# Attention of one query over a long cache: keys loaded and scored one pair ahead of the values

## The chip, the core and the metric

The kernel runs on one core of one Trainium2 chip. The metric is the time of the kernel on the device in microseconds (us), as the median of several runs. A profile is one further execution that was recorded; its span, from the first to the last instruction, is a little shorter than the time of a run.

The engines have short names in what follows: PE multiplies matrices and transposes them, DVE, ACT and POOL work elementwise (ACT also computes the exponentials, POOL the reductions over partitions), and SP issues the loads. SP's loads form one queue, which 16 DMA engines serve in order.

## What is computed

There are 32 query heads of one position each, and 8 heads of keys and values with 65536 positions of 128 numbers; four query heads share one head of keys and values. In bf16, keys and values are 134 MB each.

```python
B, Hq, Hkv, Sq, Sk, D = 1, 32, 8, 1, 65536, 128
k = jnp.repeat(k, rep, axis=1)
v = jnp.repeat(v, rep, axis=1)
scores = jnp.einsum("bhqd,bhkd->bhqk", q, k) * D ** -0.5
p = jax.nn.softmax(scores, axis=-1)
return jnp.einsum("bhqk,bhkd->bhqd", p, v)
```

## The kernel before

**Tiling.** A head's 65536 positions are cut into four units of 128 tiles; a tile is 128 positions by 128 numbers. Two units make a *pair*, so there are 16 pairs, two to a head, numbered p = 0 to 15 (`NP`). The keys of a pair, K(p), are 8 MB, and so are its values, V(p). A unit within a pair is called n = 0 or 1.

**Buffers.** `kbuf` holds the keys of a whole pair (64 KB on each partition), `bbuf` those of one unit. `vbuf` holds the values of one pair; there is one such buffer. `pts` holds the exponentials of a unit (one buffer for each n), `qkb` in PSUM the scores of a unit, `pvb` the sums of values.

**What happens to a pair.** For each of 16 groups of 8 tiles PE transposes the keys (L135), DVE or ACT copies the transposes from PSUM to `ktb` (L207, L205), and PE multiplies them with the four queries (L144), three groups behind the transposes. Unit 1 is read from `bbuf`: while PE works on unit 0, POOL copies six and ACT two sixteenths-of-a-pair from the second half of `kbuf` to `bbuf` (`copy_unit`, L213), so that `kbuf` comes free early. When a unit's scores are complete, DVE takes the maximum over its positions (L225), POOL takes it over the partitions (L393), DVE forms the new running maximum (L235, L236, L243), and ACT the exponentials with their sums (L347) and the factor alpha by which what was summed so far has to shrink (L351). Then PE multiplies the exponentials with the values (`pe_values`, L162): 128 matmuls for each unit, one group of accumulation in PSUM for each, in `pvb[0]` and `pvb[1]`. DVE adds each group to `acc` (L257, L259). At the end of a head the sum of the exponentials is reduced on POOL (L395), and the quotient is written (L309; L305 in the last head).

**The order of the work** is written out by hand, engine by engine, with semaphores. On PE a lap of the loop is the transposes and scores of both units, and then the values of both units of the same pair (`pe_pair`). On SP the order is K0, V0, K1, V1, ..., K15, V15. Three semaphores hold loads back:

- `kfree` (L411, L418, L428, L407): K(p) waits until unit 0 of pair p-1 is transposed and unit 1 copied to `bbuf`: three counts a pair.
- `bfree`: keys that are loaded straight into `bbuf` (pairs 0, 14 and 15, which are loaded by units; the others, `WHOLE`, are loaded as a whole) wait until unit 1 of the pair before is transposed.
- `vfree` (L437, or L407 for the last pair's pieces): V(p) waits until PE is done with the values of pair p-1. DVE counts it up when the last group of values is complete (`pvd`).

K0 is loaded in four pieces and V15 in five (128, 73, 38, 13 and 4 tiles), each with a semaphore of its own; all other values have one semaphore for the whole load. In the last lap of PE, L155 adds `acc` to the last group by a matmul with the identity, so that only the quotient is left after it.

Of the kernel before, what the change touches and what calls it, by code (L numbers as in the profile page):

```python
# [5 lines left out]
DT = mybir.dt  # L6
# [24 lines left out]
WHOLE = (1, 14)  # L31
# [20 lines left out]
def bass_standalone__gqa_softmax__decode_kernel(nc, q, k, v, out):  # L52
# [32 lines left out]
    cmax = sb("cmax", [P, R], DT.float32)  # L85
# [5 lines left out]
    rsum = sb("rsum", [P, R], DT.float32)  # L91
# [25 lines left out]
    acr, l_sem, lws = sem("acr"), sem("l_sem"), sem("lws")  # L117
    xd, xa, xg = sem("xd"), sem("xa"), sem("xg")
# [19 lines left out]
    def pe_scores(pe, n, j):  # L138
        take(pe, eva if on_act(j) else evd)
        if n == 0 and j == 0:  # L140
            take(pe, qrdy)
        for i in range(TB):
            t, off = j * TB + i, (j % NKG * TB + i) * P
            ins = pe.matmul(qkb[n][:, t * R:(t + 1) * R], lhsT=ktb[:, off:off + P],  # L144
                            rhs=qcur[:, :], start=True, stop=True)
        if j == G - 1:
            ins.then_inc(qkd, 1)

    def pe_values(pe, n, lap):
        vv = vbuf[:, n * T * D:(n + 1) * T * D].rearrange("p (t d) -> p t d", d=D)  # L150
        for t in range(T):
            if n and t == V_PIECES[1][0]:
                with pe.If(lap == NP - 1):
                    pe.wait_ge(acr, H)
                    pe.matmul(pvb[n][:, 0:R], lhsT=identf[:, :], rhs=acc[:, :], start=False, stop=False)  # L155
            if t == 0:
                take(pe, vp[n][0], 16)
                take(pe, exd)
# [3 lines left out]
            ins = pe.matmul(pvb[n][:, 0:R], lhsT=vv[:, t, :], rhs=pts[n][:, t * R:(t + 1) * R],  # L162
                            start=t == 0, stop=t == T - 1)
            if piece:
                pe.sem_inc(piece, -16)
        ins.then_inc(pvd, 1)

    def pe_pair(pe, lap):
# [9 lines left out]
        for n in range(2):  # L178
            pe_values(pe, n, lap)
# [44 lines left out]
    def chunk_max(e, n):  # L224
        e.tensor_reduce(cmax[:, :], qkb[n][:, :].rearrange("p (t g) -> p g t", g=R),  # L225
                        AX.X, ALU.max).then_inc(cm, 1)

    def new_max(e, n, fresh):
        take(e, cma)

        mn, mo = m[n], m[1 - n]

        def newer(to):
            if fresh:
# [4 lines left out]
        if fresh:  # L239
            newer(mn).then_inc(dmr, 1)  # L240
        else:
            own(e, newer(mn), xd)
            e.tensor_tensor(dm[:, :], mn[:, :], mo[:, :], ALU.subtract).then_inc(dmr, 1)  # L243

    def rescale(e, n, fresh):
        take(e, sx)
        if fresh:
            own(e, e.tensor_copy(lp[:, :], rsum[:, :]), xd)
        else:
            own(e, e.tensor_tensor(acc[:, :], acc[:, :], alpha[:, :], ALU.mult), xd)  # L250
            own(e, e.tensor_tensor(lp[:, :], lp[:, :], alpha[:, :], ALU.mult), xd)
            own(e, e.tensor_tensor(lp[:, :], lp[:, :], rsum[:, :], ALU.add), xd)

    def values_done(e, n, fresh):
        e.wait_ge(pvd, 1)
        if fresh:
            own(e, e.tensor_copy(acc[:, :], pvb[n][:, 0:R]), xd)  # L257
        else:
            own(e, e.tensor_tensor(acc[:, :], acc[:, :], pvb[n][:, 0:R], ALU.add), xd)  # L259
        e.sem_inc(pvd, -1)  # L260

    def dve_pair(e, second, lap):

        fresh, last = not second, second
        for j in range(G):
            if not on_act(j):
                evict(e, 0, j)
            if j == 0:
                e.sem_inc(pgo, 1)
        for j in (0, 1, 2):  # L270
            evict(e, 1, j)
        take(e, qkd)
        chunk_max(e, 0)
        evict(e, 1, 4)
        new_max(e, 0, fresh)
        for j in (5, 6, 8, 9, 10):
            evict(e, 1, j)
        rescale(e, 0, fresh)
        if fresh:
            own(e, e.tensor_copy(otmp[:, 0:HR - R], oT[:, R:HR]), xd)  # L280
            own(e, e.tensor_copy(oT[:, 0:HR - R], otmp[:, 0:HR - R]), xd)
            e.transpose(orow[:, :], oT[:, :]).then_inc(t_o, 1)
        for j in (12, 13, 14):
            evict(e, 1, j)
        take(e, qkd)
        chunk_max(e, 1)
        new_max(e, 1, False)
        if last:
# [3 lines left out]
        values_done(e, 0, fresh)  # L292
        rescale(e, 1, False)
        if not last:
            e.wait_ge(pvd, 1)
            e.sem_inc(vfree, 1)
            values_done(e, 1, False)
            return
        e.sem_inc(acr, 1)
# [3 lines left out]
        with e.If(lap == H - 1):  # L303
            e.wait_ge(pvd, 1)
            e.tensor_tensor(oT[:, HR - R:HR], pvb[1][:, 0:R], recip[:, :], ALU.mult).then_inc(t_f, 1)  # L305
        with e.Else():
            e.wait_ge(pvd, 1)
            e.sem_inc(vfree, 1)
            own(e, e.tensor_tensor(acc[:, :], acc[:, :], pvb[1][:, 0:R], ALU.add), xd)  # L309
            e.tensor_tensor(oT[:, HR - R:HR], acc[:, :], recip[:, :], ALU.mult).then_inc(t_f, 1)  # L310
        e.sem_inc(pvd, -1)
# [16 lines left out]
    def vector_engine(e):  # L328
# [6 lines left out]
        with e.Fori(0, H) as lap:  # L335
            dve_pair(e, False, lap)
            dve_pair(e, True, lap)
        e.wait_ge(s_x, 2)
# [3 lines left out]
    def exps(e, n):  # L342
        take(e, ng)
        sv = qkb[n][:, :].rearrange("p (t g) -> p g t", g=R)
        pv = pts[n][:, :].rearrange("p (t g) -> p g t", g=R)
        for g in range(R):
            ins = e.activation(pv[:, g, :], sv[:, g, :], AF.Exp, bias=negm[:, g:g + 1],  # L347
                               scale=scale, accum_out=rsum[:, g:g + 1])
        ins.then_inc(exd, 1)
        take(e, dmr)  # L350
        e.activation(alpha[:, :], dm[:, :], AF.Exp, scale=1.0).then_inc(sx, 1)  # L351

    def act_pair(e, lap):
# [10 lines left out]
        for j in (3, 7):  # L364
            evict(e, 1, j)
        exps(e, 0)
        for j in (11, 15):
            evict(e, 1, j)
        exps(e, 1)

    def scalar_engine(e):
# [3 lines left out]
        e.activation(identf[:, :], ident[:, :], AF.Copy).then_inc(t_if, 1)  # L375
        with e.Fori(0, NP) as lap:
# [3 lines left out]
    def gpsimd_engine(e):  # L380
# [3 lines left out]
        with e.Fori(0, H) as lap:  # L384
            for u in range(HU):
                if u % 2 == 0:
                    take(e, pgo)
                    lo, hi = ((w - u // 2 + 1) // 2 for w in WHOLE)
                    cond = (lap - (lo - 1)) * (hi - lap) > 0 if lo else lap < hi
                    copy_unit(e, cond, POOL_COPIES, e.tensor_copy, cpg, xg)  # L390
                    e.sem_inc(kfree, 1)
                take(e, cm)
                e.partition_all_reduce(cmaxa[:, :], cmax[:, :], P, bass.bass_isa.ReduceOp.max).then_inc(cma, 1)  # L393
# [4 lines left out]
    def sync_engine(e):  # L398
# [14 lines left out]
        for p in range(NP):  # L413
            ks, vs = src(kf, p), src(vf, p)
# [5 lines left out]
            else:  # L420
                for n in range(2):
                    if n and p:
                        e.wait_ge(bfree, p)
                    to, s = bbuf if n else kbuf, ks[:, n * W:(n + 1) * W]
                    if p == 0 or (p == NP - 1 and n == 0):
                        pieces(to, s, K_PIECES[n], kp[n])
                    else:
                        e.dma_start(to[:, 0:W], s).then_inc(kp[n][0], 16)  # L428
                        tokens(kp[n][1:])
                e.sem_inc(cpg, len(POOL_COPIES))  # L430
                e.sem_inc(cpa, len(sum(ACT_COPIES.values(), ())))
            if p:
                e.wait_ge(vfree, p)
            if WHOLE[0] <= p < WHOLE[1]:
                tokens(kp[1])
# [6 lines left out]
        e.wait_ge(t_o, H)  # L442
# [43 lines left out]
```

## Time and profile before

| | |
|---|---|
| median of 3 runs | 628.17 us (628.1 to 628.23) |
| span of the profiled execution | 626.9 us |
| PE busy | 484.6 us, 77% |
| DVE busy | 315.1 us, 50% |
| ACT busy | 228.9 us, 37% |
| POOL busy | 159.9 us, 26% |
| queue of loads, share of the 16 DMA engines' time | 99.2% |
| read from memory | 268.44 MB, 428 GB/s over the span |

A row of the timeline or of a group names the line (L162 is line 162 of the kernel before), the engine, the operation, the tile written and the tiles read, and how many. The idle time before a row stands in brackets, with what ended it; "PEq" or "DVEq" there is the engine's own sequencer, which is also where a wait for a DMA can show. An issue of a load has as its time to landing the time until the last of its 16 parts is in. Busy time of PE says how long matmuls were under way and not that PE was at its peak.

### The profile page before, as it was taken

How to read it: one execution, taken by the hardware profiler on the slowest of the kernel's cores; microseconds unless marked ns; L12 is line 12 of the kernel's file. 1: busy time of each engine (PE TensorE's matmuls, PEld its weight loads, DVE VectorE, ACT ScalarE, POOL GpSimd, SP SyncE). 2: the span in 40 equal slices, each digit the busy share in tenths (PEclk: the TensorE clock that was granted, in tenths of full speed). 3: DMA queues.
4: the chain of work that ended last, by engine and by line, in shares of the span. 5: the costliest groups of instructions: out<-in, count | busy, mean ns of one | idle time of the engine just before them, and what ended most of it. 6: DMA issues, size and time to landing. Idle time of an engine off the chain costs nothing. (4 is left out here: it accounts for less than half of the span.)

```text
span 626.9 us, 27931 instructions
## 1 busy us (share of the span) xinstructions
PE 484.6 (77%) x12340; PEld 478.9 (76%) x12340; DVE 315.1 (50%) x699; ACT 228.9 (37%) x445; POOL 159.9 (26%) x124
## 2 busy tenths in 40 slices
PE   5752995959859498694976959679496894999698
PEld 5752995949859498694976959679496894999698
DVE  4620752817537174371734717356183562848274
ACT  2320532615335153341634407245062441624133
POOL 0000704307042070520605115060150702400000
PEclk9965875958769587695966959678596785969597
DMA  8999999999999999999999999999999999999997
GB/s 366 440 449 424 439 431 439 431 439 426 443 422 447 410 460 410 460 406 460 410 439 431 426 443 426 443 426 439 431 439 431 439 431 435 416 447 424 420 433 302
DMA packets 6280, 268.57 MB, mean 428 GB/s; under 512 B 896, under 2 KB 1024, under 8 KB 1152
## 3 DMA queue, kind: packets, MB, share of 16 engines
q1 hardware_dynamic: 6224, 268.45, 99.2%
q8 instruction: 6, 0.10, 0.1%
q10 hardware_dynamic: 48, 0.01, 0.0%
q14 instruction: 2, 0.02, 0.0%
HBM read 268.44 MB, written 0.01 MB: 428 GB/s over the span
## 5 line engine op out<-in xcount | busy, mean ns | idle before, releaser
L207 DVE COPY ktb<-trb 128x1024 bf16<-128x1024 bf16 x384 | 254.6, 689 | 177.5 <-PE trb L135 173.7
L205 ACT ACTIVATE ktb<-trb 128x1024 bf16<-128x1024 bf16 x128 | 131.0, 1023 | 352.7 <-PE trb L135 297.9
L135 PE MATMUL trb<-ident,kbuf 128*128 128x128 bf16 x2048 | 177.1, 245 | 104.7 <-PEq L49 104.6
L135 PEld LDWEIGHTS trb<-ident,kbuf 128*128 128x128 bf16 x2048 | 143.9, 111 | 105.6 <-issue 105.5
L213 POOL COPY bbuf<-kbuf 128x2048 bf16<-128x2048 bf16 x78 | 143.9, 1893 | 177.6 <-POOLq L49 177.6
L144 PE MATMUL qkb<-qcur,ktb 128*128 128x4 bf16 x4096 | 174.3, 165 | 11.8 <-PEq L49 10.3
L144 PEld LDWEIGHTS qkb<-qcur,ktb 128*128 128x128 bf16 x4096 | 155.2, 97 | 14.6 <-issue 14.6
L135 PE MATMUL trb<-ident,bbuf 128*128 128x128 bf16 x2048 | 157.0, 220 | 5.2 <-issue 3.9
L162 PE MATMUL pvb<-pts,vbuf 128*128 128x4 bf16 x4096 | 113.0, 166 | 15.2 <-PEq L49 11.0
L162 PEld LDWEIGHTS pvb<-pts,vbuf 128*128 128x128 bf16 x4096 | 111.1, 103 | 16.6 <-issue 15.6
L135 PEld LDWEIGHTS trb<-ident,bbuf 128*128 128x128 bf16 x2048 | 117.4, 97 | 5.5 <-issue 5.5
L393 POOL PARTITION_ALL_REDUCE cmaxa<-cmax x32 | 11.9, 370 | 254.1 <-POOLq L49 254.1
L347 ACT ACTIVATE pts<-qkb,negm 128x128 bf16<-128x128 f32 x128 | 50.9, 549 | 37.2 <-ACTq L49 37.2
L356 ACT ACTIVATE bbuf<-kbuf 128x2048 bf16<-128x2048 bf16 x26 | 49.5, 1902 | 0.0
L347 ACT ACTIVATION_READ_ACCUMULATOR pts<-qkb,negm 128x1 f32 x128 | 35.6, 278 | 0.0
L225 DVE TENSOR_REDUCE cmax<-qkb 128x4 f32<-128x512 f32 x32 | 22.0, 686 | 23.4 <-DVEq L49 23.4
L259 DVE TENSOR_TENSOR acc<-acc,pvb 128x4 f32<-128x4 f32 x16 | 2.5, 158 | 30.0 <-PE pvb L162 30.0
L257 DVE COPY acc<-pvb 128x4 f32<-128x4 f32 x8 | 1.3, 163 | 21.8 <-PE pvb L162 21.8
L395 POOL PARTITION_ALL_REDUCE la<-lp x8 | 3.4, 430 | 30.7 <-POOLq L49 30.7
L236 DVE SCALAR_TENSOR_TENSOR negm<-cmaxa,m 128x4 f32<-128x4 f32 x24 | 3.9, 163 | 11.7 <-DVEq L49 11.5
L351 ACT ACTIVATE alpha<-dm 128x4 f32<-128x4 f32 x32 | 7.1, 221 | 0.0
L250 DVE TENSOR_TENSOR acc<-acc,alpha 128x4 f32<-128x4 f32 x24 | 3.9, 164 | 6.1 <-DVEq L49 5.7
(44 smaller groups left out, 41.6 us busy)
## 6 DMA issues: line engine op xcount, KB each, us to landing
kbuf<-in_k_dram SPq DMA_DIRECT2D x4, 2048.0 KB, 16.3
bbuf<-in_k_dram SPq DMA_DIRECT2D x2, 4096.0 KB, 20.9
bbuf<-in_k_dram SPq DMA_DIRECT2D x2, 2048.0 KB, 19.9
kbuf<-in_k_dram SPq DMA_DIRECT2D x1, 4096.0 KB, 16.3
vbuf<-in_v_dram SPq DMA_DIRECT2D x1, 4096.0 KB, 21.9
vbuf<-in_v_dram SPq DMA_DIRECT2D x1, 2336.0 KB, 27.1
vbuf<-in_v_dram SPq DMA_DIRECT2D x1, 1216.0 KB, 29.6
vbuf<-in_v_dram SPq DMA_DIRECT2D x1, 416.0 KB, 30.1
```

Of the source, the lines that this page charges most:

```text
L135: ins = pe.transpose(trb[j % NTB][:, i * P:(i + 1) * P], kv[:, t, :], ident[:, :])
L144: ins = pe.matmul(qkb[n][:, t * R:(t + 1) * R], lhsT=ktb[:, off:off + P], rhs=qcur[:, :], start=True, stop=True)
L162: ins = pe.matmul(pvb[n][:, 0:R], lhsT=vv[:, t, :], rhs=pts[n][:, t * R:(t + 1) * R], start=t == 0, stop=t == T - 1)
L205: e.activation(dst, trb[j % NTB][:, :], AF.Copy).then_inc(eva, 1)
L207: e.tensor_copy(dst, trb[j % NTB][:, :]).then_inc(evd, 1)
L213: ins = op(bbuf[:, c * CB * D:(c + 1) * CB * D], kbuf[:, off:off + CB * D])
L225: e.tensor_reduce(cmax[:, :], qkb[n][:, :].rearrange("p (t g) -> p g t", g=R), AX.X, ALU.max).then_inc(cm, 1)
L236: return e.scalar_tensor_tensor(to[:, :], cmaxa[:, :], -scale, mo[:, :], ALU.mult, ALU.min)
L347: ins = e.activation(pv[:, g, :], sv[:, g, :], AF.Exp, bias=negm[:, g:g + 1], scale=scale, accum_out=rsum[:, g:g + 1])
L351: e.activation(alpha[:, :], dm[:, :], AF.Exp, scale=1.0).then_inc(sx, 1)
L356: return e.activation(o, i, AF.Copy)
L393: e.partition_all_reduce(cmaxa[:, :], cmax[:, :], P, bass.bass_isa.ReduceOp.max).then_inc(cma, 1)
```

## The change

The keys now run one pair ahead of the values. On PE, a lap is the keys of pair p and then the values of pair p-1; the loop has one lap more, in which only values are done. On SP the loads come as K0, K1, V0, K2, V1, ..., K15, V14, V15. Both units of a pair share one maximum (`pair_max` takes it after the scores of both) and one group of accumulation in `pvb[0]`. The semaphores follow: the scores of a new pair wait for the exponentials of the one before (`exd`, since both use `qkb`), the exponentials wait for the values of the pair before (`pfree`, since both use `pts`), and V(p) still waits for `vfree` p. K14 is now loaded as a whole, and K15 in two parts without pieces. The keys' load of a whole pair is followed on SP by the wait for `bfree`.

The core of the diff:

```diff
-WHOLE = (1, 14)
+WHOLE = (1, 15)
...
     def pe_scores(pe, n, j):
         take(pe, eva if on_act(j) else evd)
-        if n == 0 and j == 0:
-            take(pe, qrdy)
+        if j == 0:
+            take(pe, exd)
+            if n == 0:
+                take(pe, qrdy)
...
-            ins = pe.matmul(pvb[n][:, 0:R], lhsT=vv[:, t, :], rhs=pts[n][:, t * R:(t + 1) * R],
-                            start=t == 0, stop=t == T - 1)
+            ins = pe.matmul(pvb[0][:, 0:R], lhsT=vv[:, t, :], rhs=pts[n][:, t * R:(t + 1) * R],
+                            start=n == 0 and t == 0, stop=n == 1 and t == T - 1)
...
-        ins.then_inc(pvd, 1)
+        ins.then_inc(pvd if n else pfree, 1)
...
-        with pe.Fori(0, NP) as lap:
-            pe_pair(pe, lap)
-        pe.wait_ge(t_f, H)
+        with pe.Fori(0, NP + 1) as lap:
+            with pe.If(lap < NP):
+                pe_keys(pe)
+            with pe.Else():
+                pe.wait_ge(exd, 2)
+                pe.wait_ge(pvf, NP - 1)
+            with pe.If(lap > 0):
+                for n in range(2):
+                    pe_values(pe, n, lap)
+        pe.wait_ge(t_f, 1)
...
+    def pair_max(e):
+        for n in range(2):
+            take(e, qkd)
+            ins = e.tensor_reduce(cmax[:, n * R:(n + 1) * R], qkb[n][:, :].rearrange("p (t g) -> p g t", g=R),
+                                  AX.X, ALU.max)
+        own(e, ins, xd)
+        e.tensor_tensor(cmaxp[:, :], cmax[:, 0:R], cmax[:, R:2 * R], ALU.max).then_inc(cm, 1)
...
+    def values_done(e):
         e.wait_ge(pvd, 1)
+        e.sem_inc(pfree, 1)
+        e.sem_inc(vfree, 1)
         e.sem_inc(pvd, -1)
...
+        for n in range(2):
+            for j in range(G):
+                if not on_act(j):
+                    evict(e, n, j)
+                if n == 0 and j == 0:
+                    e.sem_inc(pgo, 1)
+        pair_max(e)
+        if second:
             next_queries(e)
         else:
             e.sem_inc(qrdy, 1)
+        new_max(e, second)
+        if second:
+            values_done(e)
...
-        for j in (3, 7):
+        for j in (3, 7, 11, 15):
             evict(e, 1, j)
-        exps(e, 0)
-        for j in (11, 15):
-            evict(e, 1, j)
-        exps(e, 1)
+        for n in range(2):
+            take(e, pfree)
+            exps(e, n)
+        take(e, dmr)
+        e.activation(alpha[:, :], dm[:, :], AF.Exp, scale=1.0).then_inc(sx, 1)
...
+        def keys(p):
+            ks = src(kf, p)
             if p:
                 e.wait_ge(kfree, 3 * p)
             if WHOLE[0] <= p < WHOLE[1]:
                 e.dma_start(kbuf[:, :], ks).then_inc(kp[0][0], 16)
                 tokens(kp[0][1:])
+                e.wait_ge(bfree, p)
+                tokens(kp[1])
+                return
...
+        def values(p):
+            vs = src(vf, p)
             if p:
                 e.wait_ge(vfree, p)
             if p < NP - 1:
                 e.dma_start(vbuf[:, :], vs).then_inc(vp[0][0], 16)
                 tokens(vp[1])
             else:
                 for n in range(2):
                     pieces(vbuf[:, n * W:(n + 1) * W], vs[:, n * W:(n + 1) * W], V_PIECES[n], vp[n])
+
+        for p in range(NP):
+            keys(p)
+            if p:
+                values(p - 1)
+        values(NP - 1)
```

More of the change, by code (lines that the diff above doesn't have):

```diff
@@ L238, in new_max @@
         newer(negm).then_inc(ng, 1)
-        if fresh:
+        if not second:
             newer(mn).then_inc(dmr, 1)
@@ L291, in dve_pair @@
             e.sem_inc(qrdy, 1)
[L292 to L297, printed above, removed]
+        new_max(e, second)
+        if second:
+            values_done(e)
+            own(e, e.tensor_copy(acc[:, :], pvb[0][:, 0:R]), xd)
+            e.sem_inc(pvf, 1)
+        else:
+            with e.If(lap > 0):
+                values_done(e)
+                own(e, e.tensor_tensor(acc[:, :], acc[:, :], pvb[0][:, 0:R], ALU.add), xd)
+                e.sem_inc(pvf, 1)
+                own(e, e.tensor_tensor(oT[:, HR - R:HR], acc[:, :], recip[:, :], ALU.mult), xd)
+                own(e, e.tensor_copy(otmp[:, 0:HR - R], oT[:, R:HR]), xd)
+                own(e, e.tensor_copy(oT[:, 0:HR - R], otmp[:, 0:HR - R]), xd)
+                e.transpose(orow[:, :], oT[:, :]).then_inc(t_o, 1)
+        take(e, sx)
+        if not second:
+            own(e, e.tensor_tensor(lp[:, :], rsum[:, 0:R], rsum[:, R:2 * R], ALU.add), xd)
             return
+        own(e, e.tensor_tensor(acc[:, :], acc[:, :], alpha[:, :], ALU.mult), xd)
+        own(e, e.tensor_tensor(lp[:, :], lp[:, :], alpha[:, :], ALU.mult), xd)
+        for n in range(2):
+            own(e, e.tensor_tensor(lp[:, :], lp[:, :], rsum[:, n * R:(n + 1) * R], ALU.add), xd)
         e.sem_inc(acr, 1)
@@ L384, in gpsimd_engine @@
         with e.Fori(0, H) as lap:
[L385 to L391, printed above, removed]
+            for second in range(2):
+                take(e, pgo)
+                lo, hi = ((w - second + 1) // 2 for w in WHOLE)
+                cond = (lap - (lo - 1)) * (hi - lap) > 0 if lo else lap < hi
+                copy_unit(e, cond, POOL_COPIES, e.tensor_copy, cpg, xg)
+                e.sem_inc(kfree, 1)
                 take(e, cm)
-                e.partition_all_reduce(cmaxa[:, :], cmax[:, :], P, bass.bass_isa.ReduceOp.max).then_inc(cma, 1)
+                e.partition_all_reduce(cmaxa[:, :], cmaxp[:, :], P, bass.bass_isa.ReduceOp.max).then_inc(cma, 1)
             take(e, lrd)
@@ L419, in sync_engine @@
                 tokens(kp[0][1:])
[L420 to L431, printed above, removed]
+                e.wait_ge(bfree, p)
+                tokens(kp[1])
+                return
+            for n in range(2):
+                if n and p:
+                    e.wait_ge(bfree, p)
+                to, s = bbuf if n else kbuf, ks[:, n * W:(n + 1) * W]
+                if p == 0:
+                    pieces(to, s, K_PIECES[n], kp[n])
+                else:
+                    e.dma_start(to[:, 0:W], s).then_inc(kp[n][0], 16)
+                    tokens(kp[n][1:])
+            e.sem_inc(cpg, len(POOL_COPIES))
+            e.sem_inc(cpa, len(sum(ACT_COPIES.values(), ())))
+        def values(p):
+            vs = src(vf, p)
             if p:
                 e.wait_ge(vfree, p)
-            if WHOLE[0] <= p < WHOLE[1]:
-                tokens(kp[1])
             if p < NP - 1:
```

87 lines of the change are left out of this document (19 added, 68 removed).

## The prediction

> **What bounds the kernel now.** I read the page first, for the share of each resource, then the chain that ended last, then the DMA issues with their times to landing, and last the timeline of the queue that issues them.
>
> ```profile
> span 626.9 us, 27931 instructions
> PE 484.6 (77%) x12340; PEld 478.9 (76%) x12340; DVE 315.1 (50%) x699; ACT 228.9 (37%) x445; POOL 159.9 (26%) x124
> q1 hardware_dynamic: 6224, 268.45, 99.2%
> 22.00:584.00 562.00, 431.99 (x10980) 427.01 (x10977) 282.29 (x616) 210.94 (x408) 157.99 (x115) 0.77 1.00 433
> 622.00:624.00 2.00, 2.00 (x62) 2.00 (x60) 0.20 (x2) 0.00 (x0) 0.43 (x1) 0.50 0.53 188
> ```
>
> The queue of loads keeps the 16 DMA engines busy for 99.2% of the span. The two stretches below it (core 0; the last two columns are DMA share and GB/s) say where the missing 0.8%, 5.0 us, lies: from 22 to 584 us the share is 1.00, and only the last microseconds fall off. So the loads are the bound, in every lap: 268.45 MB at 433 GB/s is 620 us, and the rest of the span is the start, the tail and at most a few tenths of pauses. No other engine is over 77%. A change of order cannot make the bytes fewer; it can only keep the queue full, or let it run empty. The question is therefore one for each load in the new order: is it issued before the loads ahead of it have landed?
>
> The issue of each load is a wait on SP, and these waits are long now:
>
> ```profile
> SPq L418 <- POOLq L391: 236.1, 12, 20.9
> SPq L411 <- DVEq L296: 141.6, 7, 34.0
> SPq L411 <- DVEq L308: 108.3, 6, 18.4
> SPq L437 <- DVEq L308: 8.3, 1, 8.3
> ```
>
> They cost nothing, since another load is in flight meanwhile. L411 and L437 are values waiting for their buffer (`vfree`, counted up when the values of the pair before are done); L418 is keys waiting for `kfree`. What covers a wait of V(p) is the load of K(p) just ahead of it. That is what to follow through the change.
>
> The end of the run, from SP's timeline and the DMA issues (KB each, median us from issue to landing of all 16 parts):
>
> ```profile
> 579.88 0.33 SPq L428 DMA_DIRECT2D bbuf<-in_k_dram  x1
> 592.83 2.23 SPq L407 DMA_DIRECT2D vbuf<-in_v_dram  x5
> bbuf<-in_k_dram SPq DMA_DIRECT2D x1, 4096.0 KB, 25.1
> vbuf<-in_v_dram SPq DMA_DIRECT2D x1, 27.2
> vbuf<-in_v_dram SPq DMA_DIRECT2D x1, 4096.0 KB, 21.9
> vbuf<-in_v_dram SPq DMA_DIRECT2D x1, 128.0 KB, 29.9
> 558.27 0.33 SPq L437 DMA_DIRECT2D vbuf<-in_v_dram  x1
> 585.78 6.96 PE L162 MATMUL pvb<-pts,vbuf 128*128 128x4 bf16 x256 [4.34 <-PEq L49]
> ```
>
> V14, issued at 558.27, lands at 558.27 + 27.2 = 585.47. PE starts its values 0.31 us later and takes 6.96 us, to 592.74; SP issues the five pieces of V15 at 592.83, 0.09 us after that. Meanwhile K15 is in flight: its last half lands at 579.88 + 25.1 = 604.98. So V15 is issued 12 us before the queue would run dry, its first half (4096 KB) lands at 592.83 + 21.9 = 614.73, 9.75 us behind K15, and its last piece, issued at 594.6, at 594.63 + 29.9 = 624.53. From K15's landing to V15's last piece: 19.55 us, pure transfer.
>
> **The change part by part.** *The order of loads.* K15 moves ahead of V14, and the last three loads are K15, V14, V15. The values still have one buffer, `vbuf`, filled by the whole pair, and V15 still waits for `vfree` 15, that is for the values of pair 14. But V14 is now the load just ahead of V15. PE can't start on V14 before it has landed, since one semaphore covers the whole load; SP can't issue V15 before PE has gone through all 256 matmuls. Nothing is left to transfer meanwhile. In all other places a K stands between two V, as before; this one place has lost its cover.
>
> The price, by the steps that the trace shows for just this handover. The bytes up to and with V14 are those up to and with K15 before, so V14 lands at 604.98. Then 0.31 to PE's start, 6.96 for the values, 0.09 to SP's issue: V15 is issued at 612.34. An empty queue has to start again, and the only such start with data is the first load of the run:
>
> ```profile
> kbuf<-in_k_dram SPq DMA_DIRECT2D x1, 2048.0 KB, 7.3
> 0.72 0.88 SPq L407 DMA_DIRECT2D kbuf<-in_k_dram  x2
> qsb<-in_q_dram ACTq DMA_DIRECT2D x1, 8.0 KB, 4.3
> 625.77 0.25 SPq L448 DMA_DIRECT2D out_dram<-lrow  x1
> ```
>
> 7.3 us for 2048 KB, where a stream in motion takes half of the 9.75 us of 4096 KB, 4.87: a restart costs 2.43 us. Behind it the 19.55 us of V15. The last piece lands at 612.34 + 2.43 + 19.55 = 634.32 instead of 624.53: **+9.79 us**. The trace never shows the queue empty in its middle, so the restart has two ends: below, the last output, 1 KB issued at 625.77 into an idle queue and over with the span at 626.9, 1.1 us in all; above, the query load, 8 KB that takes 4.3 us as it shares the engines with K0. I take the 2.43, since it is the same kind of load in the same size of parts, and keep 1.1 and 4.3 for the range.
>
> [...]
>
> *The 6.96 us.* Does PE do these 256 matmuls faster when it isn't just waking up? The rows for two clocks:
>
> ```profile
> 585.00:593.00 8.00, 7.20 (x259) 7.17 (x260) 0.76 (x5) 0.00 (x0) 0.00 (x0) 0.50 1.01 432
> 617.25 3.44 PE L162 MATMUL pvb<-pts,vbuf 128*128 128x4 bf16 x128
> 617.30:619.60 2.30, 2.30 (x93) 2.30 (x94) 1.24 (x6) 0.46 (x3) 0.37 (x1) 0.94 0.99 418
> ```
>
> At a granted clock of 0.50 it is 6.96 / 256 = 27 ns each, at 0.94 it is 3.44 / 128 = 27 ns. So the clock makes no difference; 6.9 to 7.2 (a lap below) are the ends.
>
> *Are the keys of pair 15 done in time?* They stand before V14's values in PE's order. Before, PE's last scores end at 617.29, 12.3 us after the last half of K15 landed:
>
> ```profile
> 616.95 0.34 PE L144 MATMUL qkb<-qcur,ktb 128*128 128x4 bf16 x8 [0.52 <-PEq L49]
> 617.44 0.69 DVE L225 TENSOR_REDUCE cmax<-qkb 128x4 f32<-128x512 f32 x1 [1.49 <-DVEq L49]
> 619.23 0.16 DVE L243 TENSOR_TENSOR dm<-m 128x4 f32<-128x4 f32 x1
> ```
>
> Now K15 lands a load earlier, at 585.47, its keys end near 597.8, and V14 lands at 604.98: 7.2 us to spare. The exchange of the maximum through POOL, which stands ahead of `values_done` on DVE, took until 619.39, 2.1 us after the last scores; with a second reduction of 0.69 and the maximum of the two it is an estimated 3 us. It fits, so DVE stands ready to count `vfree` up. The exponentials of pair 15 now wait for `pts` (`pfree`), and run while V15 is in flight, 19.55 us of cover.
>
> *The middle laps.* V(p) now waits for values p-1, which follow keys p on PE. One lap before:
>
> ```profile
> 410.00:412.00 2.00, 0.60 (x7) 0.64 (x8) 0.00 (x0) 0.00 (x0) 0.00 (x0) 0.50 1.06 459
> 434.93 7.18 PE L162 MATMUL pvb<-pts,vbuf 128*128 128x4 bf16 x256
> 442.32 0.33 SPq L437 DMA_DIRECT2D vbuf<-in_v_dram  x1
> 424.14 0.33 SPq L418 DMA_DIRECT2D kbuf<-in_k_dram  x1
> 450.09 2.19 PE L135 MATMUL trb<-ident,kbuf 128*128 128x128 bf16 x19 [7.99 <-PEq L49]
> kbuf<-in_k_dram SPq DMA_DIRECT2D x1, 25.8
> ```
>
> PE begins the keys at 411.4 (0.60 us of PE in the first row), the values at 434.93, V is issued at 442.32, and the next K lands at 424.14 + 25.8 = 449.9 (PE starts at 450.09). The new lap has the same keys and values back to back, so V is issued about then, 7.6 us before the queue would be dry, 5.2 over the restart. The maxima, the exponentials (one round less of POOL and DVE) come in PE's 7.99 us of idle time. They are worth nothing, as PE, DVE and ACT wait for loads there; at most the 5.0 us of missing share less start and tail, some 0.5 us, could be won. K(p) still waits for `kfree` alone, by POOL's copies, as before.
>
> *The start.* K1 follows K0 directly, and V0 stands behind a wait for `bfree` 1 on SP.
>
> ```profile
> 19.68 0.33 SPq L418 DMA_DIRECT2D kbuf<-in_k_dram  x1
> 36.23 1.02 ACT L205 ACTIVATE ktb<-trb 128x1024 bf16<-128x1024 bf16 x1 [3.08 <-ACTq L49]
> 2.94 0.33 SPq L437 DMA_DIRECT2D vbuf<-in_v_dram  x1
> vbuf<-in_v_dram SPq DMA_DIRECT2D x1, 40.6
> 31.69 0.40 PE L135 MATMUL trb<-ident,bbuf 128*128 128x128 bf16 x4 [3.87 <-issue]
> ```
>
> K1 can be issued at 19.68, when the first half of K0 is through PE; nothing in that path changes but two waits that are met. K0's first quarter lands at 0.72 + 7.3 = 8.02, three more take 3 x 4.87: 22.6. That leaves 2.95 us, 0.5 over the restart: no pause, but close. V0 is issued once the last tile of K0 is transposed, at 36.2; K1 then lands where V0 did, 2.94 + 40.6 = 43.5: 4.9 us over the restart. Both at nothing; if K1 were 1 us late, it would cost 0.5.
>
> *The tail.* Last landing to the end of the span was 626.9 - 624.53 = 2.4 us, of 4 matmuls, the quotient, a transpose, a copy and the output. These stay. The second accumulation group is gone, but lay before it.
>
> Sum: span 626.9 + 9.8 = 636.7. The runs' median is 628.17, 1.27 over the profiled span; with the same surroundings, **637.9 us**.
>
> **The rivals.** *V15 isn't held* (not slower). Place: SP's wait ahead of V15. If `vfree` 15 came 2.43 us before V14's landing, the queue would stay full, and the time would be 628.2. For it: the same wait cost nothing before. Against: PE needs the landed V14. 3%.
>
> *The loads run faster in the new order.* The page's slices show between 406 and 460 GB/s:
>
> ```profile
> GB/s 366 440 449 424 439 431 439 431 439 426 443 422 447 410 460 410 460 406 460 410 439 431 426 443 426 443 426 439 431 439 431 439 431 435 416 447 424 420 433 302
> ```
>
> From 433 to 443 in the mean would be 14 us less and outweigh the pause: 624. Against: low and high slices stand side by side around one mean, whatever is loaded. 2%.
>
> *A second pause at the start* (slower still): K1 late, or a stall of PE like the 3.87 us it shows up to 31.69, put down to its own issue and not to a semaphore, but earlier. Price 1 to 4 us: 639 to 642. For it: 0.5 us of slack. Against: nothing in the path has grown. 10%.
>
> *V is late in each lap*: PE would have to lose 5.2 us a lap, and each microsecond over it costs 14. 650 and up. 3%.
>
> **How the numbers follow.** 82% for the one pause, 637.9. Its own range is from a restart of 1.1 and values of 6.9 (1.33 and 0.06 us less: 636.5) to a restart of 4.3 and values of 7.2 (640.0). With the tenths that a single profile leaves open, the range is 636.3 to 640.2; it takes in the shorter half of the second pauses and leaves out some 12%. Over 0.2%, 1.3 us (about what a measurement can tell from no change), slower: 82 + 10 + 3 = 95%; same 3%, faster 2%.
>
> **What would show it.** In the changed profile: DMA share near 0 for some 9 us about 605 to 614 us; SP's issue of V15 some 7.4 us after V14's landing, not before it; V15's first half landing about 12.2 us after its issue; share 1.00 elsewhere, with K1 issued near 19.7; keys of pair 15 ended before V14 lands. Wrong would be: V15 issued with V14 in flight, a gap at 21 us, or one in each lap.

## The result and the profile after

The changed kernel took 639.84 us as the median of five runs (637.92 to 640.88), against 628.17 us for the kernel before (628.04 to 628.26): 1.0179 times as long, with a 95% interval of 1.0164 to 1.0194. (A ratio, here and below, need not be the quotient of the two medians beside it.) The profiled execution is one of the shorter runs, with 638.14 us and a span of 636.7 us. So there are two things to explain: the 9.8 us by which the profiled span grew, and a spread of 3 us between runs, where the five of the kernel before lie within 0.3 us.

The page of the kernel after, with its head, the DMA share and GB/s in 40 slices, the queue of loads and the chain that ended last:

```profile
span 636.7 us, 27790 instructions
PE 485.4 (76%) x12340; PEld 480.8 (76%) x12340; DVE 306.1 (48%) x608; ACT 234.1 (37%) x431; POOL 165.2 (26%) x114
DMA  9999999999999999999999999999999999999847
GB/s 370 445 431 446 424 432 428 432 453 420 441 424 432 445 424 449 420 436 424 437 445 424 441 428 432 432 428 453 420 441 424 432 441 428 445 414 447 358 198 330
...
q1 hardware_dynamic: 5936, 268.45, 97.8%
...
DMA 3%; PE 1%; SPq 0%; issue 0%; DVE 0%; DVEq 0%
```

The bytes are the same, PE is as busy as before, and DVE has 9 us less to do. The queue's share fell from 99.2% to 97.8%, and the loss stands in the last three slices: 358, 198 and 330, where the kernel before ended with 420, 433 and 302. The chain that ended last now holds a transfer of values (DMA 3%, 19.8 us of V15's transfer), where before it held only PE's last matmuls and the steps behind them.

The handover from V14 to V15, from SP's waits (us, times, longest), the timelines of SP and PE, two answers on DMA issues (KB, us to landing), and stretches (the last columns are granted clock, DMA share, GB/s):

```profile
SPq L400 <- DVEq L260: 33.6, 1, 33.6
578.01 0.33 SPq L433 DMA_DIRECT2D vbuf<-in_v_dram  x1
vbuf<-in_v_dram SPq DMA_DIRECT2D x1, 26.9
605.08 6.97 PE L165 MATMUL pvb<-pts,vbuf 128*128 128x4 bf16 x256 [3.44 <-PEq L49]
612.23 2.33 SPq L400 DMA_DIRECT2D vbuf<-in_v_dram  x5
vbuf<-in_v_dram SPq DMA_DIRECT2D x1, 4096.0 KB, 12.1
...
22.00:600.00 578.00, 454.42 (x11484) 450.64 (x11482) 290.98 (x559) 224.11 (x406) 163.68 (x106) 0.78 1.00 433
604.50:613.00 8.50, 6.97 (x256) 6.91 (x256) 0.16 (x1) 2.37 (x13) 0.00 (x0) 0.50 0.00 0
```

V14 lands at 578.01 + 26.9 = 604.91. PE had waited 3.44 us for it, starts at 605.08 and works 6.97 us. SP issues V15 at 612.23, and the first half of V15 lands 12.1 us later, at 624.3, against 9.75 us of pure transfer for that half. From 604.5 to 613 us the DMA share is 0.00: the queue is empty for the whole of PE's work. Before that, from 22 to 600 us, the share is 1.00 at 433 GB/s, as in the kernel before. SP's wait for `vfree` ahead of V15 was 8.3 us before and is 33.6 us now; its length isn't what it costs, since most of it lies beside V14's transfer, but its end is.

### The profile page after: what moved, and what is told of

Read it like the earlier page. It is cut to its first block, busy times and chain, and to the rows that moved or that the text cites. A ratio compares the mean times of both kernels' runs of the same rounds, so it can differ in the third digit from the quotient of the medians.

```text
span 636.7 us, 27790 instructions
## 1 busy us (share of the span) xinstructions
PE 485.4 (76%) x12340; PEld 480.8 (76%) x12340; DVE 306.1 (48%) x608; ACT 234.1 (37%) x431; POOL 165.2 (26%) x114
## 3 DMA queue, kind: packets, MB, share of 16 engines
q1 hardware_dynamic: 5936, 268.45, 97.8%
## 5 line engine op out<-in xcount | busy, mean ns | idle before, releaser
L137 PE MATMUL trb<-ident,kbuf 128*128 128x128 bf16 x2048 | 179.8, 246 | 110.1 <-PEq L49 110.1
L213 ACT ACTIVATE ktb<-trb 128x1024 bf16<-128x1024 bf16 x128 | 131.1, 1024 | 278.9 <-PE trb L137 226.3
L137 PEld LDWEIGHTS trb<-ident,kbuf 128*128 128x128 bf16 x2048 | 145.6, 111 | 111.0 <-issue 111.0
L221 POOL COPY bbuf<-kbuf 128x2048 bf16<-128x2048 bf16 x84 | 155.1, 1897 | 128.3 <-POOLq L49 128.3
L148 PEld LDWEIGHTS qkb<-qcur,ktb 128*128 128x128 bf16 x4096 | 156.8, 97 | 15.9 <-issue 15.6
L165 PE MATMUL pvb<-pts,vbuf 128*128 128x4 bf16 x4096 | 111.1, 166 | 20.9 <-PEq L49 20.6
L386 POOL PARTITION_ALL_REDUCE cmaxa<-cmaxp x16 | 5.9, 371 | 247.7 <-POOLq L49 247.7
L347 ACT ACTIVATE bbuf<-kbuf 128x2048 bf16<-128x2048 bf16 x28 | 53.3, 1902 | 0.0
L284 DVE TENSOR_TENSOR acc<-acc,pvb 128x4 f32<-128x4 f32 x7 | 1.1, 158 | 36.3 <-DVEq L261 36.3
L294 DVE TENSOR_TENSOR acc<-acc,alpha 128x4 f32<-128x4 f32 x8 | 1.3, 162 | 11.6 <-DVEq L49 11.6
## 6 DMA issues: line engine op xcount, KB each, us to landing
vbuf<-in_v_dram SPq DMA_DIRECT2D x1, 4096.0 KB, 12.1
vbuf<-in_v_dram SPq DMA_DIRECT2D x1, 1216.0 KB, 19.8
```

The lines of the kernel that those rows point to most:

```text
L137: ins = pe.transpose(trb[j % NTB][:, i * P:(i + 1) * P], kv[:, t, :], ident[:, :])
L165: ins = pe.matmul(pvb[0][:, 0:R], lhsT=vv[:, t, :], rhs=pts[n][:, t * R:(t + 1) * R], start=n == 0 and t == 0, stop=n == 1 and t == T - 1)
L213: e.activation(dst, trb[j % NTB][:, :], AF.Copy).then_inc(eva, 1)
L221: ins = op(bbuf[:, c * CB * D:(c + 1) * CB * D], kbuf[:, off:off + CB * D])
L347: return e.activation(o, i, AF.Copy)
L386: e.partition_all_reduce(cmaxa[:, :], cmaxp[:, :], P, bass.bass_isa.ReduceOp.max).then_inc(cma, 1)
```

## The experiments

All kernels are edits of the changed kernel; `...` in a diff stands for lines that aren't shown. A time is the median of four to twelve runs, beside runs of the kernel before on the same chip, whose medians were 628.16 to 628.32 us. Of 60 such runs of the kernel before 56 lie between 628.0 and 628.5 us and four at 629.3 to 629.5.

### The changed kernel again

> The changed kernel once more, nothing edited: what is asked is where its runs part from each other (637.9 to 640.9 us, against 628.0 to 628.3 for the kernel before). Theory of the start: SP issues K1 when the first half of K0 is through PE, 20.36 us in the profiled run, about 2 us before K0 has landed on the fastest engines (22.2 us); in the longer runs PE is later there by some microseconds, and the queue is empty between K0 and K1. Then a profile of a long run shows K1 issued later than 21 us and a DMA share under 1 near 22 to 25 us. Rival: the pause ahead of V15 itself varies; then a long run has it longer than the 8.7 us of the first profile. Time under both: 637.9 to 641.

Five runs: 637.94 us in the median, 637.87 to 640.48 (1.0169 times the kernel before, 1.0156 to 1.0182). Four lie within 1 us, and one is 2.5 us longer, so the spread is the kernel's. The profile that it left was of a short run again (span 636.5 us), with K1 issued at 19.92 and K2 at 57.42. This run alone doesn't tell the theories apart, and no long run of the changed kernel itself left a profile. The long runs that did are of the edited kernels below.

### Half of the wait

```diff
...
             take(e, pfree)
+            if n == 0:
+                e.sem_inc(vhalf, 1)
...
-            if p:
+            if 0 < p < NP - 1:
                 e.wait_ge(vfree, p)
...
                 for n in range(2):
+                    e.wait_ge(vfree if n else vhalf, p + 1 - n)
                     pieces(vbuf[:, n * W:(n + 1) * W], vs[:, n * W:(n + 1) * W], V_PIECES[n], vp[n])
```

> The first half of V15 waits for the first half of V14's values alone (128 of the 256 matmuls); its other pieces wait for all of them, as before. V14 is still loaded as a whole with one semaphore. Theory of the pause (landing, PE's start, matmuls, issue, restart, one after the other): the pause gets shorter by 128 matmuls of 27 ns, 3.5 us; span about 633.2 us where the start doesn't lose anything, V15 issued some 3.9 us after V14 has landed. Rival (the pause is mostly the restart of the queue, and PE's work hides beside it): under 1 us is won.

The four runs were 634.79 to 637.13 us (636.95 in the median, 1.014 times the kernel before, 1.0126 to 1.0155); three of them are long. The profiled run is the short one, so it is compared with the short profiles of the changed kernel: its span is 633.2 us, 3.3 to 3.5 us under theirs. SP's and PE's timelines:

```profile
605.21 6.96 PE L165 MATMUL pvb<-pts,vbuf 128*128 128x4 bf16 x256 [3.50 <-PEq L49]
608.90 5.26 SPq L402 DMA_DIRECT2D vbuf<-in_v_dram  x5
```

V15 is issued 3.69 us after PE's start, and 7.15 us in the kernel after: 3.46 us less, which is half of PE's 6.96, and the span is shorter by as much. PE's work doesn't hide beside the restart; it stands in a row with it.

### Both halves, V14 loaded in two

```diff
-                e.dma_start(vbuf[:, :], vs).then_inc(vp[0][0], 16)
-                tokens(vp[1])
+                if p < NP - 2:
+                    e.dma_start(vbuf[:, :], vs).then_inc(vp[0][0], 16)
+                    tokens(vp[1])
+                else:
+                    for n in range(2):
+                        e.dma_start(vbuf[:, n * W:(n + 1) * W], vs[:, n * W:(n + 1) * W]).then_inc(vp[n][0], 16)
+                    tokens(vp[1][1:])
```

This stands beside the edit of the half.

> V14 too is loaded in two halves with a semaphore each, and each half of V15 waits for the values of the same half of V14. PE then works on one half while the other is in flight (9.7 us of transfer against 3.5 of matmuls). Theory of the pause: it is gone, the queue stays full from V14 to V15, and the span is about 627 us, the time about 628, where the start loses nothing; with the loss of the long runs up to 631. Rival (the changed order is slower for another reason than V15's wait, in the laps or at the start): it stays near 637.

632.84 us in the median (630.99 to 633.98; 1.0068 times the kernel before, 1.0055 to 1.0081), with a profiled span of 632.1. Better by some 5 us, and worse than expected by as much. Two things were missed, and both can be read. First, from SP and PE:

```profile
603.50 0.34 PE L148 MATMUL qkb<-qcur,ktb 128*128 128x4 bf16 x8 [0.69 <-PEq L49]
604.02 5.14 PE L165 MATMUL pvb<-pts,vbuf 128*128 128x4 bf16 x190 [0.18 <-PEq L49]
607.65 5.26 SPq L402 DMA_DIRECT2D vbuf<-in_v_dram  x5
```

The first half of V14 had been there since 597 us, but PE stood in the keys of pair 15 until 603.8 and came to its values only then. V15 was issued at 607.65, when V14 had already landed. So a pause of some 3 us stayed (0.8 from V14's landing at 606.8 to the issue, and the restart), set by the keys and not by the load. (At 603.50 PE's last scores of pair 15 begin; the row is 0.34 us long. V14's halves were issued at 580.04 and 580.45 and landed 17.1 and 26.4 us later.) Second, this profile is of a long run, with K2 issued at 59.74 us instead of 57.4; that is the next question.

### K1's second half at once

```diff
+            if p == 1:
+                e.dma_start(kbuf[:, W:2 * W], ks[:, W:2 * W]).then_inc(ksec, 16)
             if p:
                 e.wait_ge(kfree, 3 * p)
+            if p != 1:
+                e.sem_inc(ksec, 16)
+            if p == 1:
+                e.dma_start(kbuf[:, 0:W], ks[:, 0:W]).then_inc(kp[0][0], 16)
...
```

PE takes `ksec` ahead of its first keys of each pair.

> The second half of K1 goes into the half of kbuf that nothing uses in pair 0, so it needs no wait and is issued at the start; the first half of K1 is issued where K1 was, with 9.7 us of transfer ahead of it. Theory of the start: all runs are now short ones, 637.5 to 638.3 us, and their spread is below 0.6 us. Rival (the spread comes from the pause ahead of V15 or from elsewhere): the runs still reach from 637.9 to 640.9.

The runs: 640.01, 637.66, 639.68, 637.75, 637.75 us (1.016 times the kernel before, 1.0147 to 1.0173). The spread stays, so K1 alone isn't its cause. But the profiled run is the longest one, and it shows another place: K2 was issued at 60.12 us. Two profiles show it side by side. The first row of each is from PE's timeline (its first keys of pair 1); then come SP's issue of K2, its time to landing, and the stretch from 57 to 66 us.

The kernel after, a short run:

```profile
44.72 3.57 PE L137 MATMUL trb<-ident,kbuf 128*128 128x128 bf16 x32 [7.95 <-PEq L49]
57.36 0.33 SPq L411 DMA_DIRECT2D kbuf<-in_k_dram  x1
kbuf<-in_k_dram SPq DMA_DIRECT2D x1, 25.0
57.00:66.00 9.00, 9.00 (x227) 9.00 (x225) 6.91 (x11) 3.88 (x4) 0.13 (x1) 1.00 1.08 466
```

The kernel with both halves, a long run:

```profile
47.09 3.15 PE L137 MATMUL trb<-ident,kbuf 128*128 128x128 bf16 x28 [9.27 <-PEq L49]
59.74 0.33 SPq L413 DMA_DIRECT2D kbuf<-in_k_dram  x1
kbuf<-in_k_dram SPq DMA_DIRECT2D x1, 24.4
57.00:66.00 9.00, 9.00 (x228) 9.00 (x226) 7.12 (x11) 4.05 (x4) 2.50 (x2) 1.00 0.97 386
```

K2 is issued 12.64 us after PE's start in the one and 12.65 in the other; POOL's six copies are 11.08 of it in both. But the start differs by 2.4 us, with K1 landed at 43.7 and at 43.5. K2 then lands at 82.4 and at 84.1, and from 57 to 66 us 386 GB/s were moved instead of 466: over 9 us that is 0.72 MB, or 1.7 us at 433 GB/s.

Why 59.74 is too late shows when the landing of V0, the load ahead, is taken apart. The last of its 16 parts is in at 63.1 and 62.9 us, but the first at 61.0 and 60.9 and half of them by 61.4 and 61.3, so the engines don't run dry all at once. At 59.74 there are 3.2 us to the last part and only 1.6 to the time when half are in, less than the restart of 2.4 us.

By the profile no other engine ends PE's wait (it is put down to PE's own sequencer); PE's code is the candidate. The queue of instructions (q8; 6 packets and 0.10 MB in the whole profile of the kernel after, 16 KB each), in the stretches 40 to 43 us of the kernel after and 43 to 46 us of the other:

```profile
q8 instruction: 1, 0.02, 2.4%
```

```profile
q8 instruction: 1, 0.02, 2.3%
```

The packet that comes at 41.42 us in the short run comes at 43.80 in the long one, and PE starts 2.2 us after its end in both (42.55 and 44.91). In all eight profiles of kernels with this jump in which PE starts more than 0.7 us after K1's landing, it starts 2.1 to 2.5 us after the end of such a packet. In the two others, `kbuf_k1` and `k1_cover` below, the packet has ended by 41.1 us, and PE starts 0.3 us after the landing. In lap 0 PE jumps over the block of values to the loop's end and back, which the kernel before never does. The profile doesn't name the engine whose code a packet of q8 holds; that it is PE's is supported by an edit of PE's program alone, `peel` below, with which q8 has 39 packets instead of 6.

### V15 into another buffer

```diff
-            if p:
+            if 0 < p < NP - 1:
                 e.wait_ge(vfree, p)
...
-                    pieces(vbuf[:, n * W:(n + 1) * W], vs[:, n * W:(n + 1) * W], V_PIECES[n], vp[n])
+                    if n:
+                        e.wait_ge(kfree, 3 * NP)
+                    pieces(kbuf[:, (1 - n) * W:(2 - n) * W], vs[:, n * W:(n + 1) * W], V_PIECES[n], vl[n])
```

`vl` is a set of semaphores for V15; PE's values of pair 15 read `kbuf` and stand behind the loop.

> V15 goes into kbuf, which keys of pair 15 leave free early, with semaphores of its own; it no longer waits for the values of pair 14. PE does the last pair's values after the loop, from kbuf. Theory of the pause: the queue stays full from V14 to V15, and 9.3 us go: span 627.2 where K2 is issued in time (57.4 us), 629 to 629.5 where PE starts the second lap late and K2 is issued near 60 us; times 628.4 and 630.5. Rival (something else in the changed order costs the time): over 633.

The profiled span is 626.8 us; twelve runs, 628.16 to 633.06, 628.44 in the median, 1.0022 times the kernel before (1.0007 to 1.0037). SP's timeline, and the stretch in which the queue had been empty:

```profile
577.93 0.33 SPq L435 DMA_DIRECT2D vbuf<-in_v_dram  x1
578.54 13.09 SPq L402 DMA_DIRECT2D kbuf<-in_v_dram  x5
...
604.50:613.00 8.50, 6.96 (x256) 6.91 (x256) 0.16 (x1) 2.51 (x13) 0.00 (x0) 0.50 1.00 430
```

PE does the same 256 matmuls in the same place, and the DMA share beside them is 1.00 instead of 0.00. V15 has another buffer and another wait, and the last pair's values stand elsewhere in PE's code; nothing else has changed, and 9.7 us of span are back (636.5 to 626.8). Seven of twelve runs are at 628.2 to 628.5, the other five at 630.4 to 633.1, so the spread doesn't come from V15's wait.

### The keys of pair 0 ahead of the loop

```diff
-        with pe.Fori(0, NP + 1) as lap:
-            with pe.If(lap < NP):
-                pe_keys(pe)
...
+        pe_keys(pe)
+        with pe.Fori(0, NP - 1) as lap:
+            pe_keys(pe)
+            for n in range(2):
+                pe_values(pe, n, False, [vbuf[:, 0:T * D], vbuf[:, T * D:2 * T * D]])
```

The last pair's values stand behind the loop.

> PE does the keys of pair 0 ahead of the loop, so that it doesn't jump over the block of values in the first lap and back to the loop's start; loads, waits and buffers stay as in the changed kernel, V15's wait too. Theory of the jump (PE's code for the second lap arrives late, PE starts K1's keys at 44.7 or at 47.1 us, and K2 is issued at 57.4 or 59.7 us, the second of which is too late): PE now starts K1's keys within 0.5 us of K1's landing (43.7 us), K2 is issued near 56.5 us, all runs are short ones (637.5 to 639 us) with a spread below 0.8 us; some more code is fetched once. Rival (PE starts late for another reason, the waits on the exponentials for instance): the spread of some 2.5 us stays.

679.42 us in the median (1.0781 times the kernel before, 1.0741 to 1.0821): a miss by some 41 us, in the wrong direction. The part that it was made for came out: PE starts K1's keys at 43.56 us and K2 is issued at 56.20. But:

```profile
q8 instruction: 39, 0.64, 0.4%
...
DMA  9999779999999999779999699999999999699856
```

There are 39 loads of code of 16 KB instead of 6, some of them hundreds of microseconds into the loop, and the queue's share falls to 0.7 and 0.6 in the slices near them. V1 was issued at 88.73 us, and at 75.90 in the kernel after. The edit took away one late start and brought many, so it doesn't decide whether the spread goes away.

The loop issues some 1540 matmuls and weight loads a lap (12340 of each in 16 laps), and here the keys' 1024 stand once more in front of it and the values' 512 behind. With V15 in `kbuf` PE has the 512 more behind the loop too, and that profile has 8 loads of code: six by 49 us, and two from 618 us on. In this one a loop of the same length is loaded again from 241, 327 and 531 us on. Whether the length of PE's program accounts for that is not shown; why the loads come back stays open.

> Both edits together. If the pause ahead of V15 and the late start of PE's second lap are all that the changed order costs, the time is that of the kernel before, 628.2 to 629.3 us, in all runs. If the order has a third cost, it stays over 630.

With both edits, 659.71 us in the median, 651.41 to 682.2 (1.0439 times the kernel before by the three shortest runs, interval 1.0402 to 1.0476). There are 30 loads of code, so this run can't say whether there is a third cost.

### Cover ahead of K2

```diff
+            if p == 2:
+                e.dma_start(fill[:, :], src(vf, 1)[:, 0:40 * D]).then_inc(fsem, 16)
             keys(p)
```

On top of V15 in `kbuf`; `fill` is read by nobody.

> Beside V15 in kbuf (628.2 to 628.5 us in its short runs, 630.4 to 633.1 in its long ones), a useless load of 10 KB a partition into a spare buffer is issued just ahead of K2's wait, as cover: 1.31 MB, an estimated 3.0 us of transfer at 433 GB/s, in all runs. Theory of K2 (the long runs issue K2 some 2.4 us later, after the queue's restart time has begun, since PE starts the second lap late): lateness up to 3 us is covered, the runs are 631.2 to 631.6 us with a spread below 0.8 us, but for a rare one that is later still. Rival (the spread comes from elsewhere): the runs reach from 631.3 to 636, as far apart as before.

632.31 us in the median, 631.31 to 633.27 (1.006 times the kernel before, 1.0047 to 1.0072): the spread shrank from 4.9 to 2.0 us and didn't go. The profiled run is a long one, and shows why. The rows are K1's issue and time to landing in the changed kernel, the two narrow places in this run (K1 with its time to landing, and K2), and the stretch from 18 to 26 us in it:

```profile
20.36 0.33 SPq L411 DMA_DIRECT2D kbuf<-in_k_dram  x1
kbuf<-in_k_dram SPq DMA_DIRECT2D x1, 23.4
...
20.58 0.33 SPq L415 DMA_DIRECT2D kbuf<-in_k_dram  x1
kbuf<-in_k_dram SPq DMA_DIRECT2D x1, 24.7
60.26 0.33 SPq L415 DMA_DIRECT2D kbuf<-in_k_dram  x1
18.00:26.00 8.00, 6.46 (x161) 6.34 (x157) 4.62 (x7) 2.96 (x3) 0.00 (x0) 1.00 1.05 422
```

K2 is issued as late as 60.26, but now the useless load is in flight. The time was lost earlier: K1, issued at 20.58, landed at 45.3, and in the kernel after, issued at 20.36, at 43.8. From 18 to 26 us 422 GB/s were moved; in the run with both places covered, below, it is 457. Of K0's last load the first part is in at 22.3 here, half by 22.5 and the last at 24.0, so K1 was issued 1.9 us before half of them were.

### Two more sixteenths for ACT

```diff
-POOL_COPIES = (0, 1, 2, 3, 4, 5)
-ACT_COPIES = {3: (6,), 7: (7,)}
+POOL_COPIES = (0, 1, 2, 3, 4)
+ACT_COPIES = {3: (5,), 7: (6, 7)}
```

On top of V15 in `kbuf`.

> Beside V15 in kbuf, POOL copies five sixteenths of a pair and ACT three (six and two before), so that kbuf comes free some 0.9 us earlier in each lap (POOL ends 1.9 us earlier, ACT then ends last). Theory of K2: short runs stay at 628.2 to 628.5, the long ones get shorter by about 0.9 us (629.5 to 632). Rival (K2's wait isn't what decides): the long runs stay at 630.4 and over.

628.54 to 632.82 us, 630.03 in the median (1.0029 times the kernel before, 1.0015 to 1.0043). In the profiled run PE started at 47.34 and K2 was issued at 60.95, 13.6 us later instead of 12.6: ACT, which has its own evictions to do between the copies, was last and later than POOL had been. The edit didn't free `kbuf` earlier, so it tests nothing. More runs are long than with 6 and 2 (ten of twelve are over 628.6 us), and the profiled one lost time at both places: K1, issued at 20.87, landed at 44.8.

### Both narrow places covered

K1's second half at once, the useless load ahead of K2, and V15 in `kbuf`:

> V15 in kbuf, the useless load ahead of K2 as cover (3.0 us), and K1's second half issued at the start. Theory of two narrow places (a long run has lost time between K0 and K1, with K1 issued after 20.5 us, or between V0 and K2, with K2 issued after 58 us, or at both): both are covered now, and all runs are 631.2 to 631.6 us with a spread under 0.6 us, whether PE starts its second lap early or late. Rival (there is a third place, or the code of PE costs otherwise): the runs reach 632.5 or more.

The runs: 631.35, 631.48, 631.29, 631.36, 631.59 (1.0049 times the kernel before, 1.0035 to 1.0063). The spread is 0.3 us, and the time is that of the short runs, 628.3, plus the 3.0 of the useless load.

```profile
18.00:26.00 8.00, 6.79 (x167) 6.67 (x165) 4.96 (x8) 2.83 (x3) 0.00 (x0) 1.00 1.07 457
```

Without the useless load:

> V15 in kbuf, and K1's second half issued at the start, without the useless load: the place between K0 and K1 is covered, that between V0 and K2 is not. Theory of two narrow places: short runs of 628.2 to 628.5 and long ones of 629.5 to 630.6, none of 631.5 or more. Rival (K1's place alone makes the long runs): all are below 628.8.

Eleven runs, 628.21 to 630.46, 629.88 in the median (1.0021 times the kernel before, 1.0012 to 1.003): three at 628.2 to 628.4, the other eight at 629.1 to 630.5, none above. Without a cover the spread was 4.9 us, with K1 covered it is 2.2, with K2 covered 2.0, and with both 0.3. So the two places make the spread.

The ten profiles of kernels with the jump in PE's first lap give a measure of "in time". Ten times a K1 or a K2 without cover was issued at least 2.1 us before half of the parts of the load ahead were in; it landed 19.3 to 20.0 us behind that load's last part. Five times it was issued only 1.4 to 1.9 us before; it landed 20.3 to 21.3 us behind.

## Why the prediction was right, and where it was not

The time forecast, 637.9 us, lies 1.9 us under the median of the first five runs and at that of the five after them (637.94), and 639.84 is inside the range of 636.3 to 640.2. The profiled span, 636.7 us, is the one worked out. That the first median stayed in the range is partly luck: three of those five runs carry a second loss, which the forecast put at nothing, and two of them, 640.37 and 640.88, lie above it.

**The pause ahead of V15** (+9.79 us forecast): shown. V14's landing was 604.91 (604.98 forecast), PE's start 0.17 us later (0.31), its work 6.97 us (6.96), V15's issue 612.23 (612.34), the restart 12.1 - 9.75 = 2.35 us (2.43). The span grew by 9.8 us. That the wait for the buffer is the cause, and not the order of loads as such, is shown by V15 in `kbuf` (9.7 us back) and by half of the wait (3.5 us back). The clock of 0.50 in the pause changed nothing: 27 ns for each matmul (6.97 us for 256), as in the kernel before at 0.50 (6.96 us for 256) and at 0.94 (3.44 us for 128).

**The keys of pair 15**: forecast to end near 597.8 with 7.2 us to spare; they ended at 601.6, with 3.3.

```profile
570.93 6.91 PE L165 MATMUL pvb<-pts,vbuf 128*128 128x4 bf16 x256 [0.18 <-PEq L49]
578.01 3.57 PE L137 MATMUL trb<-ident,kbuf 128*128 128x128 bf16 x32 [0.18 <-PEq L49]
601.30 0.34 PE L148 MATMUL qkb<-qcur,ktb 128*128 128x4 bf16 x8 [0.68 <-PEq L49]
```

The prediction counted 12.3 us from the landing of K15's last half, but PE comes to these keys straight from the values of pair 13, at 578.01, and needs 23.6 us for them; PE is the bound there and not the load. It made no difference to the time, and it is what kept a pause in the kernel with both halves.

**The middle laps** (nothing won, nothing lost): right in the profile after, with a share of 1.00 from 22 to 600 us. The 9 us that DVE saves are worth nothing.

**"K(p) still waits for `kfree` alone, by POOL's copies, as before"**: the step that was mis-sized, at K2. The wait is the same, but what lies ahead of it isn't checked there: K2 has one V0 for cover, PE's start and 12.6 us of work to wait for and 2.4 us of restart. In the short run K2 is issued 5.7 us before the last part of V0 is in and about 4 before half of its parts are. In the long run of the kernel with both halves PE started 2.4 us later than that: K2 was issued 1.6 us before half of V0's parts were in, 386 GB/s were moved instead of 466, and K2 landed 1.7 us later. The prediction worked out such a slack for V in the middle and for K1, V0 and not for K2.

**The start** ("no pause, but close"): half right. The profiled run has none, as forecast; K1 was issued at 20.36 us (19.68 forecast), and K0, forecast to land at 22.6, had half of its last parts in by 22.5 and the last one at 24.1. The slack was small enough that the place costs 1.5 us of K1's landing in the profile with the cover ahead of K2, with K1 issued at 20.58. So the rival of a second pause at the start, with 1 to 4 us and 10%, came true in part: by the experiments with covers it is what lifts the median of the first five runs from the 637.9 that was forecast to 639.84. It was looked for at K1 and in a stall of PE, and it stands at K1 and at K2.

The other rivals fell: V15 was held, the rate stayed 433 GB/s, and V is issued in time in each lap.

That the late start of PE comes from its code is supported by the packets' times in ten profiles and by the earlier start without the jump (43.56 us, 0.1 us after K1's landing), and not shown by an edit that changes only that. Why the packet comes at 41.4 in one run and 43.8 in another stays open. No version beat the kernel before: its queue was full (99.2%), so the best that the new order can do is to come back to 628.2 us.

## What to carry to other kernels

Where loads are the bound, a new order of loads is judged place by place: for each load that waits for a buffer, what is in flight while its consumer works, and how much of it is left when the wait ends. Here what was left counted to the time when half of the parts of the load ahead were in and not to the last part, some 1.6 us later (22.5 and 24.1 us for K0's last load, 61.4 and 63.1 for V0): K1 and K2 landed 19.3 to 20.0 us behind the last part where they were issued at least 2.1 us before that time, and 20.3 to 21.3 where it was 1.4 to 1.9. An order that is safe in the middle of the loop can lack cover at its ends, where the two streams no longer alternate; here two loads of the same kind fell side by side, on one buffer. And one profile with a full queue isn't enough where the slack is smaller than the spread of an engine's start: PE's start of pair 1 differed by 2.4 us between two profiles (44.72 and 47.09 us), and K2 was in time in one of them only.

## What was not expected of the hardware

With the keys of one pair repeated ahead of the loop, code was loaded again from 241, 327 and 531 us on: 39 loads of 16 KB instead of 6, and some 41 us over the changed kernel (679.42 against 637.94 us), though the loop itself is as long as before; why stays open. In the kernels with a jump over the values in the first lap PE started its second lap 0.3 to 4.0 us after its keys had landed, in eight of ten profiles 2.1 to 2.5 us after the end of a packet of code. And loads that started on an empty queue took an estimated 2.4 us beyond their transfer: 2.35 for V15 in the kernel after (12.1 - 9.75) and 2.43 for K0 at the start of the kernel before (7.3 - 4.87).
